# Attention and two MoE layers on one core: weight loads moved behind batch 0's first 256 rows, and the stacked 64-row block transposed once per pair of heads

## The chip, the cores and the metric

The kernel runs on one core of a Trainium2 chip. The metric is device time in microseconds (us), the median of several executions of the compiled program; lower is better.

## What is computed

```python
# q, k, v: (4, 8, 576, 64), f: (4, 8, 576)
scores = q @ k.T / 8
cum = cumsum(log(clip(f, 1e-4, 1)))
scores = where(causal, -1e9, scores + cum[:, None] - cum[None, :])
attn = softmax(scores) @ v
x = attn as (2304, 512)
y = relu(x @ w_in) ** 2 @ w_out        # 512 -> 2048 -> 512
out = elu(y @ w2_in) @ w2_out
```

## The kernel before

Each batch has 8 heads in 4 pairs. A head's 576 rows are five blocks of at most 128, and the work of a pair is cut into steps: two "A" steps (one per head: rows 0 to 255, two blocks), a "4" step (the last 64 rows of both heads, stacked into one block of 128 rows), and two "B" steps (one per head: rows 256 to 511). In batch 0 all eight A steps come first, then "4", "B", "B" for each pair; in the others a pair's five steps follow each other (`todo`, line 651). The loop of line 709 issues step i's scores and softmax (`soft`) and the transposes and products with v of step i - 1 (`outs`).

Batch 0 is computed in full fp32 (`Plain`); the others split each operand in two fp32r parts, so a product is two or three matmuls. The probabilities are transposed on TensorE against an identity (`tr`, line 397), copied out of PSUM (`split_pt`, line 393, by ACT and VectorE) and multiplied with v (`av`, line 400). `out_b` (line 464) does this for a B step: for each 128-column piece J (`turn`, line 473) it transposes the stacked block `e4`, and the head's two blocks in `e`. The stacked block holds both heads, 64 rows each; the identity has 192 columns, and a shift of its columns by 64 puts the half of the current head next to the head's other blocks:

```python
tr(pt[:, 0:128], e4[:, j], last)     # last = 64 * (1 - k)
tr(pt[:, 128:256], e[:, j])
tr(pt[:, 256:384], e[:, 512 + J * 128:640 + J * 128])
```

So both heads of a pair transpose all five pieces of `e4`. `out_a` (line 443) multiplies a second block padded with zeros to 256 columns, `out_b` a fourth one padded to 256.

Beside the attention runs the first half of the first MoE layer. Its rows go in units of 256 (`unit`, line 591): a unit is 18 small steps, 8 of the first product (`ph`), 8 of the second (`o`), and two others. `moe_step` (line 683) issues the next one; a credit of `PACE[b] * COST[kind]` steps per attention step says how often. Unit 0 takes batch 0's first 256 rows and can start when batch 0's A steps are done. All MoE matmuls are issued on line 176 (`mm3`).

The weights arrive as fp64 and are converted on the chip (`load_w`, line 143): 16 halves of 512 KB, first the eight of `w_in`, then the eight of `w_out`. `stage` (line 133) issues the DMA on SP's queue; then ACT takes the absolute value (line 156), VectorE assembles the bits in four operations (lines 157 to 160), ACT rounds to fp32r (line 163) and POOL subtracts for the low part (line 128). `W_AT` (line 36) says how many halves are issued at step i of the loop: one each in steps 0 to 3, two each in steps 8 to 13. The first five DMAs go out at step 0 (line 721).

The decay (`cum`, line 215) is added inside the score matmul: its rows `ca` are written to partitions 64 to 67 of the query and key tiles by DMAs of ACT's queue (line 257). The order of instructions on each engine is then set by the tile framework's scheduler.

Of the kernel before, what the change touches and what calls it, by code (L numbers as in the profile page):

```python
# [10 lines left out]
F32 = mybir.dt.float32  # L11
# [24 lines left out]
W_AT = (1, 1, 1, 1, 0, 0, 0, 0, 2, 2, 2, 2, 2, 2)  # L36
# [14 lines left out]
FOLD = 'vv'  # L51
# [9 lines left out]
BUFS = {'raw': 3, 'qs': 3, 'vv': 4, 'ea': 2, 'eb': 3, 'p': 4, 't': 2, 'x': 1, 'xh': 1}  # L61
# [17 lines left out]
def attention_then_moe_kernel(ctx, tc, first, firstv, plain, qkv, aug0, f, w1, w2, out):  # L79
# [18 lines left out]

    ident = const.tile([128, 192], F32, name="ident")
    make_identity(nc, ident[:, 0:128])  # L100
    nc.gpsimd.tensor_copy(ident[:, 128:192], ident[:, 0:64])
# [28 lines left out]
    staged = []  # L130
# [12 lines left out]
    def load_w(src, m, fc, wp, i, late):  # L143
# [17 lines left out]
        if not late:  # L161
            stage()
# [38 lines left out]
    ptA = [[a1.tile([128, 512], F32R, name=f"ptA{s}{t}") for t in range(2)] for s in range(2)]  # L201
    ptB = [[a1.tile([128, 320], F32R, name=f"ptB{s}{t}") for t in range(2)] for s in range(2)]
    e4s = [a1.tile([128, 640], F32, name=f"e4_{s}") for s in range(2)]
# [21 lines left out]
    for s in range(2):  # L225
        for t in range(2):
            me.memset(f32(ptA[s][t][:, 384:512]), 0.0)
            nc.gpsimd.memset(f32(ptB[s][t][:, 256:320]), 0.0)
        nc.gpsimd.memset(e4s[s][:, S:640], 0.0)
# [148 lines left out]
    def soft_4(b, hp, hhs):  # L378
        e = e4s[hp % 2]
# [17 lines left out]
    def tr(dst, src, c0=0):  # L397
        seen[0] = nc.tensor.transpose(dst, src, ident[:, c0:c0 + 128])  # L398
# [8 lines left out]
    def fold(pv, n, x, c0, k, eng, hh=None):  # L407
        if isinstance(hh, Plain):
            copy(eng, x[64 * k:64 * k + 64, c0:c0 + n], pv[0:64, 0:n])
# [3 lines left out]
        if eng == "v":  # L413
            nc.vector.tensor_tensor(x[64 * k:64 * k + 64, c0:c0 + n], pv[0:64, 0:n], t[:, 0:n], op=ALU.add)
        else:
            u = ab.tile([64, 320], F32, tag="t", name="u", bufs=BUFS["t"])
            nc.scalar.activation(out=u[:, 0:n], in_=pv[0:64, 0:n], func=AF.Copy)
            nc.gpsimd.tensor_tensor(out=x[64 * k:64 * k + 64, c0:c0 + n], in0=u[:, 0:n], in1=t[:, 0:n], op=ALU.add)
# [24 lines left out]
    def out_a(hh, e, x, k):  # L443
# [13 lines left out]
        split_pt(pt[:, 0:384], hl[0][:, 0:384], hl[1][:, 0:384])  # L457
# [3 lines left out]
        av(pv[:, 0:256], hh, 1, [t[:, 256:512] for t in hl], False, True)  # L461
        fold(pv, 256, x, 0, k, FOLD[0])

    def out_b(hh, e, e4, x, k):
        last, near = 64 * (1 - k), 64 * k
        native = isinstance(hh, Plain)

        def unsplit(pt, n, J):
            p = ab.tile([128, 320], F32, tag=f"p{J % 2}", name="pp", bufs=BUFS["p"])
            copy(CP["pB"][J % 2], p[:, 0:n], pt[:, 64:64 + n])  # L470
            return [p]

        def turn(J):
            j = slice(J * 128, J * 128 + 128)
            pt = ps_t.tile([128, 512], F32, tag="t", name="pt")
            if J < 3:
                tr(pt[:, 0:128], e4[:, j], last)
                tr(pt[:, 128:256], e[:, j])
                tr(pt[:, 256:384], e[:, 512 + J * 128:640 + J * 128])
                if native:  # L480
                    return unsplit(pt, 320, J)
                hl = [ab.tile([128, 320], F32R, tag=f"p{t}", name=f"p{t}", bufs=BUFS["p"]) for t in range(2)]
                split_pt(pt[:, 64:384], hl[0], hl[1])
            else:
# [3 lines left out]
                if native:  # L488
                    return unsplit(pt, 256, J)
# [454 lines left out]
```

## Time and profile before

| | |
|---|---|
| median of 3 executions | 1054.24 us (1053.77 to 1060.94) |
| the profiled execution | 1059.11 us, its span 1057.3 us |
| TensorE matmul, weight load | 1031.7 us (98%), 877.4 us (83%) |
| VectorE, ACT, POOL | 617.1 us (58%), 492.4 us (47%), 226.6 us (21%) |

The engines are called PE (TensorE matmul), PEld (TensorE weight load), DVE (VectorE), ACT, POOL and SP as the profile does. The profiled execution holds the attention from 0 to about 372 us; what follows are the two MoE layers. Durations of matmuls overlap, since they are pipelined: how fast TensorE goes is read from the distance of starts. An fp32 matmul is two records in the trace.

### The profile page before, as it was taken

The numbers are of one execution on the slowest core, as the hardware profiler recorded it, in microseconds if no ns is written. First come the engines' busy times: TensorE is split into PE (matmuls) and PEld (weight loads), VectorE is DVE, ScalarE is ACT, GpSimd is POOL, SyncE is SP. The second block draws the span as 40 slices with busy tenths as digits, with TensorE's granted clock in tenths as the row PEclk, the third lists the DMA queues.
The fourth block names the chain that finished last, engine by engine and source line by source line (L and its number), as shares of the span: only waits on it lengthen the run. The fifth ranks groups of instructions, "written<-read, shape, count | busy, mean of one in ns | idle before, by whom it ended". The sixth has DMA issues, their size and how long they took to land.

```text
span 1057.3 us, 15495 instructions
## 1 busy us (share of the span) xinstructions
PE 1031.7 (98%) x5696; PEld 877.4 (83%) x5696; DVE 617.1 (58%) x1363; ACT 492.4 (47%) x1055; POOL 226.6 (21%) x261
## 2 busy tenths in 40 slices
PE   5999999999999999999999999999999999999998
PEld 3667798999999988889988888888888888888897
DVE  5794478766776548858875278943433433343353
ACT  4675688777786634435443154521222222222232
POOL 3457487675775200000000000000000000000000
PEclk9999999999999999999999999999999999999999
DMA  7762534543431173454747237302100300200010
GB/s 244 205 180 89 182 117 150 173 162 125 153 124 47 43 230 122 122 177 140 238 162 238 80 120 249 110 1 77 42 1 1 120 1 1 73 9 1 0 41 20
DMA packets 60112, 115.48 MB, mean 109 GB/s; under 512 B 7332, under 2 KB 34724, under 8 KB 60004
## 3 DMA queue, kind: packets, MB, share of 16 engines
q1 hardware_dynamic: 59972, 114.42, 33.5%
q8 instruction: 45, 0.74, 0.3%
q14 instruction: 31, 0.25, 0.1%
q10 hardware_dynamic: 64, 0.07, 0.0%
HBM read 87.37 MB, written 27.69 MB: 109 GB/s over the span
## 4 chain that ended last, share of the span: by engine, by line
PE 91%; DVE 4%; ACT 2%; DMA 1%; issue 1%; POOL 1%; ACTq 0%; POOLq 0%
PE O L176 32%; PE pH L176 32%; PE o L176 6%; PE ph L176 5%; PE pt L398 4%; PE pv L405 3%; PE s L326 2%; PE pv L402 2%; PE s L330 2%; PE s L331 2%; DVE wt L159 1%; PE pr L398 1%; ACT qk L119 1%; DVE wt L160 1%; DVE wt L158 1%
## 5 line engine op out<-in xcount | busy, mean ns | idle before, releaser
L176 PE MATMUL pH<-xu,w 128*128 128x512 f32 (+1 forms) x1632 | 354.0, 367 | 0.0
L176 PEld LDWEIGHTS pH<-xu,w 128*128 128x128 f32 x1632 | 283.0, 188 | 55.3
L176 PE MATMUL O<-w,gh 128*128 128x512 f32 x576 | 179.0, 394 | 0.0
L576 ACT ACTIVATE g<-g 128x512 f32<-128x512 f32 (+1 forms) x80 | 47.1, 589 | 197.0 <-DVE g L575 196.6
L176 PEld LDWEIGHTS O<-w,gh 128*128 128x128 f32 x576 | 107.2, 188 | 24.7
L176 PE MATMUL O<-gh,w 128*128 128x512 f32 (+1 forms) x448 | 122.0, 362 | 0.0
L115 DVE TENSOR_TENSOR gl<-g,gh 128x512 fp32r<-128x512 f32 (+1 forms) x136 | 85.1, 627 | 54.3 <-ACT gh L578 44.3
L176 PE MATMUL O<-w,gl 128*128 128x512 f32 x288 | 111.3, 392 | 0.0
L575 DVE TENSOR_SCALAR g<-pH 128x512 f32<-128x512 f32 (+1 forms) x80 | 51.0, 637 | 101.7 <-PE pH L176 101.6
L176 PEld LDWEIGHTS O<-gh,w 128*128 128x128 f32 x448 | 79.8, 189 | 14.2
L128 POOL TENSOR_TENSOR qk<-raw,qk 64x704 fp32r<-64x704 f32 (+1 forms) x48 | 78.8, 1642 | 20.4 <-ACT qk L119 15.2
L176 PE MATMUL O<-gl,w 128*128 128x512 f32 (+1 forms) x224 | 79.4, 363 | 0.0
L176 PE MATMUL o<-gh,w 128*128 128x256 f32 x384 | 76.6, 292 | 1.2 <-DVE xB L430 1.2
L577 DVE SCALAR_TENSOR_TENSOR g<-g,pH 128x512 f32<-128x512 f32 (+1 forms) x80 | 50.7, 634 | 45.7 <-ACT g L576 45.4
L156 ACT ACTIVATE wt<-wraw 128x512 f32<-128x512 f32 x57 | 38.0, 669 | 78.4 <-DMA wraw<-in_w_dram 69.6
L578 ACT ACTIVATE gh<-g 128x512 fp32r<-128x512 f32 (+1 forms) x80 | 47.0, 589 | 56.6 <-DVE g L577 56.6
L176 PE MATMUL ph<-xu,w 128*128 128x256 f32 x480 | 67.3, 287 | 1.6 <-DMA xu<-x 1.3
L176 PEld LDWEIGHTS O<-w,gl 128*128 128x128 f32 x288 | 54.1, 188 | 12.4
L176 PEld LDWEIGHTS ph<-xu,w 128*128 128x128 f32 x480 | 60.7, 190 | 2.5 <-DMA xu<-x 1.7
L176 PEld LDWEIGHTS o<-gh,w 128*128 128x128 f32 x384 | 60.4, 190 | 2.0 <-issue 1.4
L567 ACT ACTIVATE gh<-g 128x512 fp32r<-128x512 f32 (+1 forms) x80 | 46.6, 584 | 27.9 <-DVE g L566 23.8
L157 DVE TENSOR_SCALAR wt<-wt 128x512 f32<-128x512 f32 x64 | 29.2, 456 | 44.7 <-ACT wt L156 31.9
(132 smaller groups left out, 1694.7 us busy)
## 6 DMA issues: line engine op xcount, KB each, us to landing
wraw<-in_w_dram SPq DMA_DIRECT2D x57, 512.0 KB
raw<-in_qkv_dram SPq DMA_DIRECT2D x24, 800.0 KB
xu<-x SPq DMA_DIRECT2D x20, 512.0 KB
x<-xs SPq DMA_DIRECT2D x16, 320.0 KB
xu<-x SPq DMA_DIRECT2D x20, 256.0 KB
x<-yh SPq DMA_DIRECT2D x16, 256.0 KB
x<-yl SPq DMA_DIRECT2D x16, 256.0 KB
raws_w<-in_w_dram SPq DMA_DIRECT2D x7, 512.0 KB
```

What stands on the lines that cost most here:

```text
L115: nc.vector.tensor_tensor(dst, x, f32(hi), op=ALU.subtract)
L128: nc.gpsimd.tensor_tensor(out=dst, in0=x, in1=f32(hi), op=ALU.subtract)
L156: nc.scalar.activation(out=f32(t), in_=f32(hi), func=AF.Abs)
L157: nc.vector.tensor_scalar(f32(t), f32(t), W_MIN, W_MAX, op0=ALU.max, op1=ALU.min)
L176: nc.tensor.matmul(out=dst, lhsT=l, rhs=r, start=first and i == 0, stop=last and i == n - 1, skip_group_check=skip)
L398: seen[0] = nc.tensor.transpose(dst, src, ident[:, c0:c0 + 128])
L405: seen[0] = nc.tensor.matmul(out=dst, lhsT=hh[2][:, J, :], rhs=hl[i], start=first and i == 0, stop=last and i == 1)
L567: nc.scalar.activation(out=gh[:, 0:n], in_=g[:, 0:n], func=AF.Copy)
L575: nc.vector.tensor_scalar(g[:, 0:n], h[:, 0:n], 0.0, None, op0=ALU.min)
L576: nc.scalar.activation(out=g[:, 0:n], in_=g[:, 0:n], func=AF.Exp)
L577: nc.vector.scalar_tensor_tensor(g[:, 0:n], g[:, 0:n], -1.0, h[:, 0:n], op0=ALU.add, op1=ALU.max)
L578: nc.scalar.activation(out=gh[:, 0:n], in_=g[:, 0:n], func=AF.Copy)
```

## The change

It moves the weight loads: none in the first eight steps, then one in each of steps 8 to 23, and the first five DMAs go out at step 4. Unit 0's n-th step waits in program order until n halves are loaded, and its second product (from its ninth step) until all 16 are; before, the ninth step issued whatever was left. And it changes `out_b`: head 0 of a pair transposes the stacked block for both heads, next to its own blocks in tiles `P` of up to 640 columns: the order is [two, three, stacked | three, two], so that head 0 reads columns 0 to 319 and head 1 columns 320 to 639. Head 1 only adds its own two blocks. Head 0's result then comes in another order, and is added in three pieces (`fold`). The stacked block and the `P` tiles have one buffer each. The zero padding of the second and fourth blocks goes away.

```diff
-W_AT = (1, 1, 1, 1, 0, 0, 0, 0, 2, 2, 2, 2, 2, 2)
+W_AT = (0, 0, 0, 0, 0, 0, 0, 0, 1, 1, 1, 1, 1, 1, 1, 1, 1, 1, 1, 1, 1, 1, 1, 1)
...
     def stage():
-        if not to_stage:
+        n = n_raw[0] % 5 if n_raw[0] < 10 else n_raw[0] % 2
+        if not to_stage or n in held:
             return
         fc, i = to_stage.pop(0)
-        n = n_raw[0] % 5
         n_raw[0] += 1
+        held.append(n)
...
-    e4s = [a1.tile([128, 640], F32, name=f"e4_{s}") for s in range(2)]
+    e4t = a1.tile([128, 640], F32, name="e4t")
...
     def out_a(hh, e, x, k):
...
-        av(pv[:, 0:256], hh, 1, [t[:, 256:512] for t in hl], False, True)
+        av(pv[:, 0:128], hh, 1, [t[:, 256:384] for t in hl], False, True)
...
     def out_b(hh, e, e4, x, k):
...
         def turn(J):
-            j = slice(J * 128, J * 128 + 128)
+            if k == 0:
+                w = 640 if J < 3 else 512
+                turned[J] = [ab.tile([128, w], F32 if native else F32R, tag=f"P{J}{t}", name=f"P{J}{t}", bufs=1) for t in range(parts)]
             pt = ps_t.tile([128, 512], F32, tag="t", name="pt")
+            three_, four_ = (y[:, J * 128:J * 128 + 128] for y in (e, e4))
+            two_ = e[:, 512 + J * 128:640 + J * 128] if J < 3 else None
             if J < 3:
-                tr(pt[:, 0:128], e4[:, j], last)
-                tr(pt[:, 128:256], e[:, j])
-                tr(pt[:, 256:384], e[:, 512 + J * 128:640 + J * 128])
...
+                srcs = [two_, three_, four_] if k == 0 else [three_, two_]
             else:
...
+                srcs = [e4[:, 512:640], three_, four_] if k == 0 else [three_]
+            for i, src in enumerate(srcs):
+                tr(pt[:, i * 128:i * 128 + 128], src)
+            n = 128 * len(srcs)
+            c = slice(0, n) if k == 0 else slice(384, 384 + n)
...
-                av(pv[:, 0:320], hh, J, hl, J == 0, False)
+                av(pv[:, 0:320], hh, J, [t[:, 320 * k:320 * k + 320] for t in hl], J == 0, False)
             else:
-                n3 = 192 if native else 256
-                av(pv[:, 0:n3], hh, 3, [t[:, 64:64 + n3] for t in hl], False, False)
-                av(pv[:, 0:64], hh, 4, [t[:, 0:64] for t in hl], False, True)
-                fold(pv, 320, x, 0, k, CP["xB"] if native else FOLD[1], hh)
+                av(pv[:, 128 - 128 * k:320 - 128 * k], hh, 3, [t[:, 128 + 192 * k:320 + 192 * k] for t in hl], False, False)
+                c = 0 if k else 256
+                av(pv[:, c:c + 64], hh, 4, [t[:, 64 * k:64 * k + 64] for t in hl], False, True)
+                fold(pv, 320, x, 0, k, CP["xB"] if native else FOLD[1], hh, [(0, 0, 320)] if k else [(0, 192, 128), (128, 64, 128), (256, 0, 64)])
...
     def moe_step():
...
+            if not u and loaded[0] < (16 if n_step[0] >= 9 else n_step[0]):
+                return False
...
-            n_step[0] += 1
-            if n_step[0] == 9:
-                drain(wl)
+            if not u:
+                n_step[0] += 1
...
-        if i == 0:
+        if i == 4:
             for _ in range(5):
                 stage()
...
         for _ in range(W_AT[i] if i < len(W_AT) else 0):
             next(wl, None)
+            loaded[0] += 1
```

How this moves instructions is seen at three places. The first is the head of SP's queue (`fr` is the decay input, `rawA` the queries and keys of a pair's first 256 rows, `raws_w` and `wraw` the weights). Before:

```order
6 L255 DMA rawA<-in_first_dram 64x1024
7 L258 DMA rawA<-in_firstv_dram 128x256
8 L140 DMA raws_w<-in_w_dram 128x1024 x2
9 L140 DMA wraw_181<-in_w_dram 128x1024
10 L140 DMA wraw_183<-in_w_dram 128x1024
11 L140 DMA wraw_185<-in_w_dram 128x1024
12 L711 DMA aug<-in_aug_dram 16x2560
13 L255 DMA rawA<-in_first_dram 64x1024
```

Afterwards:

```order
6 L250 DMA rawA<-in_first_dram 64x1024
7 L253 DMA rawA<-in_firstv_dram 128x256
8 L705 DMA aug<-in_aug_dram 16x2560
9 L250 DMA rawA<-in_first_dram 64x1024
10 L253 DMA rawA<-in_firstv_dram 128x256
11 L279 DMA aug<-ca 8x2x256 x2
12 L279 DMA aug<-cp 8x2x256
13 L279 DMA aug<-cp 8x2x64
14 L279 DMA aug<-cn 8x2x320
15 L139 DMA wraw_265<-in_w_dram 128x1024
```

Five weight DMAs left the place ahead of the fourth pair's input; three now stand behind the decay rows, two more (`raws_w`) further down.

The second place is TensorE in the last two pairs of batch 0 (`pr` turns the sums of a pair, `pv` are products with v, `s` scores, `pt` transposes). Before, from the end of the third pair:

```order
122 L398 MATMUL pr<-ident,rb 128x128 x2
123 L176 MATMUL o<-gl,w_1_207 128x256
124 L326 MATMUL s<-rawB 128x384
125 L176 MATMUL o<-gh,w_2_242 128x256 x2
126 L176 MATMUL o<-gl,w_2_242 128x256
127 L176 MATMUL o<-gh,w_2_242 128x256 x2
128 L176 MATMUL o<-gl,w_2_242 128x256
129 L176 MATMUL o<-gh,w_3_294 128x256 x2
```

Afterwards, from the last `ph` of unit 0 on:

```order
106 L176 MATMUL ph<-x_116,w_7_838 128x256 x12
107 L393 MATMUL pr<-ident,rb 128x128 x2
108 L397 MATMUL pv<-P_707,vp 64x320
109 L397 MATMUL pv<-P_732,vp 64x320
110 L321 MATMUL s<-rawC 128x512
111 L397 MATMUL pv<-P_740,vp 64x320
112 L397 MATMUL pv<-P_747,vp 64x192
113 L397 MATMUL pv<-P_747,vp 64x64
114 L321 MATMUL s<-rawC 128x384
115 L393 MATMUL pt<-ident,eb 128x128 x2
```

No `o` stands between the attention's matmuls any more; the first one is in row 199, among batch 1's first pairs.

The third is TensorE in the last pair of batch 1 (`e_1` or `e4t` is the stacked block, `eb` a head's own two). Before, the transposes of one head, each piece with the stacked block:

```order
606 L398 MATMUL pt<-ident,e_1_130 128x128
607 L398 MATMUL pt<-ident,eb 128x128 x2
608 L405 MATMUL pv<-p_2368,vv 128x320
609 L405 MATMUL pv<-p_2369,vv 128x320
610 L405 MATMUL pv<-ptB_125,vv 128x256
611 L398 MATMUL pt<-ident,e_1_130 128x128
612 L398 MATMUL pt<-ident,eb 128x128 x2
```

Afterwards, those of a head 1:

```order
513 L393 MATMUL pt<-ident,eb 128x128 x2
514 L325 MATMUL s<-qk_2071 128x384
515 L326 MATMUL s<-qk_2072 128x384
516 L400 MATMUL pv<-P_2150,vv 128x320
517 L400 MATMUL pv<-P_2178,vv 128x192
518 L393 MATMUL pt<-ident,eb 128x128 x2
519 L400 MATMUL pv<-P_2179,vv 128x192
520 L400 MATMUL pv<-P_2178,vv 128x64
```

A head 1 has no transposes of the stacked block left, and its fourth block's products have 192 columns.

## Rows read from the trace of the kernel before

**Rows 1.** The page's 40 slices of the span: granted TensorE clock, in tenths.
```profile
PEclk9999999999999999999999999999999999999999
```
**Rows 2.** Stretches: start:end, length, PE, PEld, DVE, ACT, POOL busy, clock, DMA, GB/s.
```profile
46.00:88.00 42.00, 40.32 (x220) 28.50 (x219) 39.38 (x88) 31.55 (x73) 23.16 (x23) 1.00 0.51 147
88.00:129.00 41.00, 41.00 (x251) 30.40 (x249) 15.31 (x54) 22.31 (x52) 21.89 (x25) 1.00 0.47 158
131.00:208.00 77.00, 72.69 (x554) 68.56 (x554) 59.86 (x185) 64.13 (x165) 57.59 (x63) 1.00 0.43 141
208.00:284.00 76.00, 76.00 (x622) 75.27 (x621) 51.10 (x152) 57.49 (x142) 54.45 (x60) 1.00 0.45 148
```
**Rows 3.** The same stretch, 88 to 129 us, line 176 alone: PE, PEld busy.
```profile
88.00:129.00 41.00, 16.93 (x108) 13.68 (x106) 1.00 0.47 158
```
**Rows 4.** Timeline of the first 10 us: SP's and ACT's queues, VectorE.
```profile
0.74 0.39 SPq L196 DMA_DIRECT2D fr<-in_f_dram  x1
...
2.63 0.81 DVE L210 TENSOR_SCALAR fr<-fr 32x576 f32<-32x576 f32 x1 [2.63 <-DMA fr<-in_f_dram]
...
5.66 2.94 SPq L140 DMA_DIRECT2D wraw<-in_w_dram  x3
...
7.46 5.90 ACTq L257 DMA_DIRECT2D rawA<-ca  x5
```
**Rows 5.** Timeline of TensorE, 12 to 62 us: start, us, engine, line, what.
```profile
12.85 5.46 PE L326 MATMUL s<-rawA 68*128 68x256 f32 x12 [12.85 <-DMA rawA<-ca]
18.10 1.06 PE L398 MATMUL pt<-ident,ea 128*128 128x128 f32 x4
18.95 1.92 PE L326 MATMUL s<-rawA 68*128 68x256 f32 x4
...
46.51 1.63 PE L176 MATMUL ph<-x,w 128*128 128x256 f32 x6
48.07 1.54 PE L402 MATMUL pv<-ea,rawA 128*64 128x256 f32 x4
...
50.83 0.86 PE L402 MATMUL pv<-ea,rawA 128*64 128x256 f32 x4
...
54.15 0.58 PE L176 MATMUL ph<-x,w 128*128 128x256 f32 x1
...
59.19 0.27 PE L398 MATMUL pt<-ident,e 128*128 128x128 f32 x1
59.30 0.38 PE L398 MATMUL pt<-ident,eb 128*128 128x128 f32 x2
...
61.90 0.58 PE L176 MATMUL ph<-x,w 128*128 128x256 f32 x1
```
**Rows 6.** The tile `wt` of a weight load: duration min/median/max in ns.
```profile
L157 DVE TENSOR_SCALAR wt<-wt x16: 414/422/1408, 15.6 to 81.2; 128x512 f32<-128x512 f32 x16
...
L163 ACT ACTIVATE w<-wt x16: 612/629/649, 19.4 to 85.7; 128x512 fp32r<-128x512 f32 x16
L128 POOL TENSOR_TENSOR w<-wt,w x16: 1259/1272/1452, 20.5 to 86.4; 128x512 fp32r<-128x512 f32 x16
L156 ACT ACTIVATE wt<-wraw x9: 645/668/688, 21.8 to 76.0; 128x512 f32<-128x512 f32 x9
L159 DVE SCALAR_TENSOR_TENSOR wt<-wraw,wt x9: 664/694/1664, 24.4 to 79.1; 128x512 int32<-128x512 int32 x9
```
**Rows 7.** Timeline of TensorE, 215 to 235 us.
```profile
215.96 0.63 PE L405 MATMUL pv<-ptA,vv 128*128 128x256 f32 x4
216.43 0.52 PE L176 MATMUL ph<-xu,w 128*128 128x256 f32 x3
...
229.10 0.42 PE L405 MATMUL pv<-ptB,vv 128*128 128x256 f32 x3
229.36 0.55 PE L398 MATMUL pt<-ident,ea 128*128 128x128 f32 x3
```
**Rows 8.** Groups by line and form, VectorE, 120 to 380 us.
```profile
L414 DVE TENSOR_TENSOR xB<-pv,t 64x320 f32<-64x320 f32 x24 | 11.6, 482 | 7.3 <-ACT t L412 6.7
```

More of the change, by code (lines that the diff above doesn't have):

```diff
@@ L161, in load_w @@
         if not late:
+            held.pop(0)
             stage()
@@ L200, in attention_then_moe_kernel @@
     m4 = a1.tile([128, 288], F32, name="m4")
-    ptA = [[a1.tile([128, 512], F32R, name=f"ptA{s}{t}") for t in range(2)] for s in range(2)]
-    ptB = [[a1.tile([128, 320], F32R, name=f"ptB{s}{t}") for t in range(2)] for s in range(2)]
-    e4s = [a1.tile([128, 640], F32, name=f"e4_{s}") for s in range(2)]
+    ptA = [[a1.tile([128, 384], F32R, name=f"ptA{s}{t}") for t in range(2)] for s in range(2)]
+    e4t = a1.tile([128, 640], F32, name="e4t")
     me = getattr(nc, MEM)
@@ L224, in attention_then_moe_kernel @@
     split_c(ca[:, 0:2, 0:256], ca[:, 2:4, 256:512], slice(0, 256))
[L225 to L229, printed above, removed]
+    nc.gpsimd.memset(e4t[:, S:640], 0.0)
     nc.gpsimd.memset(m4, 0.0)
@@ L378, in soft_4 @@
     def soft_4(b, hp, hhs):
-        e = e4s[hp % 2]
+        e = e4t
         nm, z, r = (ab.tile([128, 1], F32, tag=t + "1", name=t + "1", bufs=3) for t in ("nm", "z", "r"))
@@ L395, in split_pt, with tr @@
         nc.vector.tensor_tensor(lo, pt, f32(hi), op=ALU.subtract)
-    def tr(dst, src, c0=0):
-        seen[0] = nc.tensor.transpose(dst, src, ident[:, c0:c0 + 128])
+    def tr(dst, src):
+        seen[0] = nc.tensor.transpose(dst, src, ident)
     def av(dst, hh, J, hl, first, last):
@@ L405, in av, with fold @@
             seen[0] = nc.tensor.matmul(out=dst, lhsT=hh[2][:, J, :], rhs=hl[i], start=first and i == 0, stop=last and i == 1)
-    def fold(pv, n, x, c0, k, eng, hh=None):
+    def fold(pv, n, x, c0, k, eng, hh=None, pieces=None):
+        rows = slice(64 * k, 64 * k + 64)
+        pieces = pieces or [(0, c0, n)]
         if isinstance(hh, Plain):
-            copy(eng, x[64 * k:64 * k + 64, c0:c0 + n], pv[0:64, 0:n])
+            for f, c, m in pieces:
+                copy(eng, x[rows, c:c + m], pv[0:64, f:f + m])
             return
@@ L412, in fold @@
         nc.scalar.activation(out=t[:, 0:n], in_=pv[64:128, 0:n], func=AF.Copy)
[L413 to L418, printed above, removed]
+        for f, c, m in pieces:
+            nc.vector.tensor_tensor(x[rows, c:c + m], pv[0:64, f:f + m], t[:, f:f + m], op=ALU.add)
     def norm_x(b, hp, kind, x, c0):
@@ L456, in out_a @@
         hl = ptA[k]
-        split_pt(pt[:, 0:384], hl[0][:, 0:384], hl[1][:, 0:384])
+        split_pt(pt[:, 0:384], *hl)
         yield
@@ L460, in out_a @@
         av(pv[:, 0:256], hh, 0, [t[:, 0:256] for t in hl], True, False)
-        av(pv[:, 0:256], hh, 1, [t[:, 256:512] for t in hl], False, True)
+        av(pv[:, 0:128], hh, 1, [t[:, 256:384] for t in hl], False, True)
         fold(pv, 256, x, 0, k, FOLD[0])
+    turned = {}
     def out_b(hh, e, e4, x, k):
-        last, near = 64 * (1 - k), 64 * k
         native = isinstance(hh, Plain)
[L468 to L471, printed above, removed]
+        parts = 1 if native else 2
@@ L492, in turn @@
-            return hl
-        hls = [turn(0)]
+                srcs = [two_, three_, four_] if k == 0 else [three_, two_]
+            else:
+                srcs = [e4[:, 512:640], three_, four_] if k == 0 else [three_]
[3 more added lines that the diff above has]
+            c = slice(0, n) if k == 0 else slice(384, 384 + n)
+            if native:
+                copy(CP["pB"][J % 2], turned[J][0][:, c], pt[:, 0:n])
+            else:
+                split_pt(pt[:, 0:n], *(t[:, c] for t in turned[J]))
@@ L495, in out_b @@
+        turn(0)
         yield
-        hls.append(turn(1))
+        turn(1)
         yield
@@ L681, in attention_then_moe_kernel @@
     n_step = [0]
+    loaded = [0]
     def moe_step():
```

24 lines of the change are left out of this document (6 added, 18 removed).

## The prediction

> **What bounds the kernel now.** The page comes first: TensorE has nearly all the busy time, and its row of granted clock is full in every slice [rows 1]. Since matmuls are pipelined, their durations overlap and a busy share near 100% doesn't say that TensorE has no room; the room shows in how often a matmul starts. So the next view is the table by stretches [rows 2]. In batch 2 (208 to 284 us) 622 records of TensorE start in 76 us, one per 0.122 us. In batch 1 (131 to 208 us) it is 554 in 77 us, one per 0.139 us, with the same kinds of instruction: 77 - 554 x 0.122 = 9.4 us of that stretch are not TensorE's. So batch 2 is bound by TensorE (I take batch 3 as like it) and batch 1 only mostly so. In batch 0 the causal blocks from row 256 on (the "B" steps) fall in two halves: from 46 to 88 us VectorE is busy for 39.4 of 42 us, and TensorE starts only 220 records; from 88 to 129 us VectorE is busy for 15.3 of 41 us and TensorE starts 251 records, 108 of them MoE matmuls of line 176 [rows 3].
>
> Third, the timeline of the start [rows 4, 5]. The decay rows `ca` are written to the query tiles by DMAs from 7.46 us on, and TensorE's first matmul waits for one of them until 12.85 us. From there TensorE is dense, but slow: four transposes take from 18.10 to 18.95 us, 0.21 us each, while from 59.19 to 59.30 us one takes 0.11. The four records of a `pv` group have a span of 1.54 us from 48.07 and 0.86 us from 50.83. The column of granted clock reads 1.00 in all of these stretches, so the level is read from the intervals: 1.2 GHz up to about 50.8 us, 2.4 GHz after. What TensorE did before it rose: 33 us of scores with 68 rows, transposes and 64-column products, almost without a gap, and then, from 46.51 us, the first MoE matmuls.
>
> **The start.** Before, five weight DMAs of 512 KB stand on SP's queue ahead of the fourth pair's input and beside the `ca` DMAs; afterwards none does until the decay rows are out. The first `ca` DMA takes 12.85 - 7.46 = 5.4 us from issue to use. A lone DMA, that of `fr`, takes 2.63 - 0.74 = 1.9 us [rows 4]. So the gain lies between 0 (if the `ca` transfers are slow by themselves) and 5.4 - 1.9 = 3.5 us. I take 3.0, near the row of the lone DMA, since the five weight DMAs are the only large traffic that goes away. The rest of the first 256 rows gains nothing: TensorE is dense there, and the four weight conversions that leave were beside it. They are what ACT, VectorE and POOL no longer do then; they come back later.
>
> **The weights.** One load costs ACT 0.67 + 0.63 us, VectorE two operations of 0.42 and two of 0.69 (2.2 us), and POOL 1.27 us [rows 6]. Of the 16 loads, before: 4 in batch 0's A steps, 12 in the first six steps of the B part (two each). Afterwards: 0, then 6 in the first two pairs of the B part, 6 in the last two, 4 in the first four steps of batch 1. The first eight MoE steps keep their places (one weight each), the other eight need all 16 loads and so move behind the 23rd step: the order shows no MoE matmul in the last two pairs of batch 0.
> - First two pairs: six loads fewer take 6 x 2.2 = 13 us from a VectorE that was busy for 39.4 of 42 us. TensorE is the next in line, and it has little room, so of the 13 I count 2.0 us (0 to 6).
> - Last two pairs: of 41 us, the 108 MoE matmuls took 108 x 0.122 = 13 us; they are not lost but run later, in a dense stretch, at the same price, so moving them costs nothing as long as the stretch gets 13 us shorter. What is left for TensorE is 28 us, less ten transposes: 27. But six loads come in: ACT 22.3 + 7.8 = 30 us (less some 2 of MoE work that leaves), VectorE 15.3 + 13.2 = 28.5, POOL 21.9 + 7.6 = 29.5 (again less 1 or 2). All four engines then need 27 to 29 us, in fixed orders, with each waiting for the others. The stretch can't be under 27 us (1 us better than neutral) and, if it stays at 41, costs 13. I take 31 us, 3.0 over neutral, because in the half before VectorE did reach 39.4 of 42 us with the same kind of mix.
> - Batch 1: four loads in its first pair, ACT 5.2 us, in a stretch where ACT, at 64 of 77 us, is not the bound [rows 2]. Cost 0 to 5.2 us; I take 1.0.
>
> **The transposes.** Before, each head of a pair transposes the five 128-column pieces of the stacked block, with an identity shifted by 64 so that its own half lands beside its other blocks. Afterwards head 0 of a pair does it for both: 5 transposes fewer per pair, 80 in all, 20 per batch. The price is the interval, 0.11 us [rows 5], not the span of one instruction (0.27 us at the same place): spans overlap. 80 x 0.11 = 8.8 us. Two matmul shapes shrink in batches 1 to 3: 48 second products of an A step from 256 columns to 128, and 48 of the fourth block from 256 to 192. Four of 256 columns take from 215.96 to 216.43, 0.118 each; the last three of a fourth block, one of 256 columns and two of 64, take from 229.10 to 229.36, so 64 columns take 0.07 [rows 7]. A 128-column one lies between; the 64-column ones look bound by something other than their columns, so I take 0.07 for 128 (saves 0.048) and 0.094 for 192 (saves 0.024): 48 x 0.048 + 48 x 0.024 = 3.5 us, bounds 0 and 4.6. In all 12.3 us of TensorE: 2.2 in batch 0, 3.4 in each of batches 1 to 3. Where TensorE bounds, that is the gain: batches 2 and 3 give 6.8 (3.4 to 6.8), the first two pairs of batch 0 give 1.1, the last two are counted above, and batch 1, with its 9.4 us of other waits, gives half: 1.7 (0 to 3.4).
>
> A rule of the Trainium skill ("TensorE: Matmul & The Clock Gate", Part 4: PE-mode transpose) puts a transpose at some 275 ns in a kernel's context; by it the 80 would be worth 22 us and the sum below 13 us lower. The timeline has that figure too, as the span of one transpose (0.27 us at 59.19), and the next one starts 0.11 us later, so the measured interval decides.
>
> **What else it moves.** The copies out of PSUM change their shapes, not their columns: per pair eight of 320 or 256 become eight of 384, 256 or 128. The last addition of head 0 is in three pieces: the one of 320 columns takes 0.48 us [rows 8], three take at most 1.4, so under 1 us of VectorE per pair, in stretches where VectorE is busy for 60 of 77 and 51 of 76 us; no cost. Two buffers become one. The stacked block `e4t` of the next pair is written by VectorE (the first row minimum) after head 0's five transposes, and the transposed `P` tiles by ACT and VectorE after head 1's products. Behind that minimum on VectorE stand copies of `P` and a weight's steps, for which TensorE and ACT wait. In batches 1 to 3 two A steps lie between; in batch 0 one step, and I take 0, bound 4 x 5 x 0.11 = 2.2 us.
>
> **The sum.** Start -3.0; first two pairs -2.0 and -1.1; last two pairs +3.0; batch 1 -1.7 and +1.0; batches 2 and 3 -6.8: -10.6 us. The rows are of an execution of 1059.1 us (span 1057.3), 0.5% above the median of 1054.2; the terms are differences of short stretches, so they are taken off the median: 1043.6 us.
>
> **Rivals.**
> - *The clock falls in the last two pairs.* There TensorE has only the mix with which it stayed at 1.2 GHz from 12.85 to 50.8 us: no MoE matmul for some 30 us. For it: that the clock did not rise for 38 us, and rose soon after the first MoE matmuls [rows 5]. Against it: between the MoE matmuls at 54.15 and 61.90 us TensorE had the same mix alone, and the transposes at 59.19 still took 0.11 us. A fall and a rise need not have one condition. Price: 27 us of TensorE at half rate are 54, 23 over the 31 taken: 1067 us. It decides as soon as the clock falls in the first half of the stretch (over 12 us more: slower than before). The Trainium skill speaks for it: the same Part 4 says that transposes do not count as TensorE being busy in the way other matmuls do; the trace agrees for the slow start and not for the 7.7 us from 54.15. Chance 0.10.
> - *The last two pairs keep their length.* Softmax, copies and loads go through three strict queues, and a chain from ACT to VectorE to ACT to POOL stands in each load; the 13 us of MoE are then only put off: +13 in place of +3, 1053.6, no change. For it: those MoE matmuls needed nothing there and were the filler of just such waits. Against it: ACT and VectorE were busy for only half of that stretch. Chance 0.17.
> - *Every bound falls well.* Start -3.5, first pairs -6 and -1.1, last pairs -1.1, batch 1 -3.4 with no cost, batches 2 and 3 -6.8: -21.9, 1032 us. For it: fillers are spread more evenly in batches 1 to 3. Against: batch 1 had room on TensorE already. Chance 0.13.
> - *My sum*, 1037 to 1050: 0.60.
>
> A measurement of this kernel can tell about 1% from no change, here 10.5 us: faster means under 1043.7. A little over half of my own case lies there (0.34) and all of the third rival (0.13): 0.47. The clock gives 0.09 beyond 1% slower; the remaining 0.44 is within 1%. The range 1032 to 1058 takes in the second rival and the lower half of the third, and leaves out the clock.
>
> **What would show it.** Right: first matmul near 9.9 us; VectorE well under 39 of 42 us in the first two pairs; the last two pairs of batch 0 in about 31 us with no line-176 matmul and transposes still 0.11 us apart; pairs of batches 2 and 3 0.85 us shorter each for the same number of MoE matmuls. Wrong: a first matmul still after 12 us, transposes 0.21 us apart after 55 us, or TensorE waiting on ACT, POOL or VectorE between batch 0 and batch 1 for more than some 6 us.

## The result, and the profile after

The changed kernel takes 1065.44 us in the median of 8 executions (1061.25 to 1069.21), the kernel before 1058.68 beside it on the same chip (8 executions); the ratio of all these executions is put at 1.0077 (that of the two medians is 1.0064), its 95% interval 1.0055 to 1.0099. So the change costs some 0.8%, where 1% faster had been forecast, and the time lies above the stated range, which ended at 1058. The profiled execution after is the fastest of its eight (1061.25 us, span 1059.4), that of before was near the top of its range, so the two traces stand only 2.1 us apart. The 97 executions of the kernel before that ran beside the experiments fall in two groups, 61 up to 1056.8 us with a mean granted clock of 0.994 to 0.998 and 36 from 1057.9 us on, half of them at 1.000, and the traced one (1059.11 us, 1.000) is of the second, so what its clock did need not hold for the others.

The first two views answer to [rows 1, 2]: the row of granted clock, and the stretches. The last two pairs of batch 0 and batch 1 are cut here at the same points of the work in both kernels. The kernel before, by these marks:

```profile
93.00:127.00 34.00, 34.00 (x211) 25.69 (x210) 12.85 (x47) 17.60 (x44) 17.44 (x19) 1.00 0.45 151
127.00:204.00 77.00, 73.16 (x551) 67.89 (x550) 59.56 (x184) 64.22 (x163) 56.25 (x61) 1.00 0.46 151
```

The kernel after, the page's row and the stretches (PE, PEld, DVE, ACT, POOL busy, granted clock, DMA share, GB/s); the first of them, 38 to 77.6 us, holds the first two pairs:

```profile
PEclk9999899999999999999999999999999999999999
...
38.00:77.60 39.60, 38.01 (x209) 26.09 (x207) 36.98 (x75) 27.55 (x65) 23.66 (x22) 1.00 0.54 163
77.60:116.00 38.40, 30.61 (x125) 17.24 (x125) 35.15 (x75) 27.73 (x68) 30.11 (x27) 0.87 0.50 165
116.00:195.00 79.00, 70.99 (x509) 64.07 (x507) 65.22 (x186) 60.93 (x156) 53.12 (x59) 0.98 0.47 155
```

The last two pairs of batch 0 now take longer (38.4 us against 34) for 125 records of TensorE instead of 211: VectorE, which had been busy for 12.85 of 34 us, is busy for 35.15 of 38.4. The clock is no longer full there (0.87). With one place on the timeline as the mark (the `pr` transposes that close a pair), the two traces compare so; the last column counts each MoE record of line 176 that a stretch has fewer (or more) than before at the 0.122 us of the prediction:

| stretch | before: us, MoE records | after | forecast | measured, MoE put off counted |
|---|---|---|---|---|
| start to the third pair of A steps | 45.80, 0 | 30.73, 0 | -3.0 | -15.1 |
| to the end of the second B pair | 47.33, 107 | 46.86, 96 | -3.1 | +0.9 |
| last two pairs of batch 0 | 33.98, 85 | 38.44, 0 | +3.0 | +14.8 |
| batch 1 | 76.91, 192 | 78.81, 180 | -0.7 | +3.4 |
| batches 2 and 3 | 166.51, 669 | 169.12, 698 | -6.8 | -0.9 |
| in all | 370.53, 1053 | 363.95, 974 | -10.6 | +3.1 |

The start, against [rows 4, 5]: the first matmul comes at 10.85 us (before 12.85), and four records of a `pv` group have a span of 1.46 us at 19.69 and 0.86 at 21.62, so in this execution the clock rises at about 21 us; before, the same pair of rows stands at 48.07 and 50.83.

```profile
7.41 4.62 ACTq L252 DMA_DIRECT2D rawA<-ca  x6
...
10.85 7.20 PE L321 MATMUL s<-rawA 68*128 68x256 f32 x16 [10.85 <-DMA rawA<-ca]
...
19.69 1.46 PE L397 MATMUL pv<-ea,rawA 128*64 128x256 f32 x4
21.62 0.86 PE L397 MATMUL pv<-ea,rawA 128*64 128x256 f32 x4 [0.47 <-ACT xA L117]
```

The weight loads, against [rows 6]: the tile `wt` from 77 to 118 us alone (minimum/median/maximum in ns). The minima are the old ones, but the medians of three of VectorE's four steps are now 0.87, 0.99 and 0.91 us, where they had been 0.42 and 0.69.

```profile
L156 DVE TENSOR_SCALAR wt<-wt x6: 403/416/1520, 77.3 to 113.4; 128x512 f32<-128x512 f32 x6
L157 DVE TENSOR_SCALAR wt<-wt x6: 417/868/1530, 77.7 to 114.6; 128x512 int32<-128x512 int32 x6
L158 DVE SCALAR_TENSOR_TENSOR wt<-raws_w,wt x6: 660/988/1314, 79.8 to 116.1; 128x512 int32<-128x512 int32 x6
L159 DVE SCALAR_TENSOR_TENSOR wt<-raws_w,wt x5: 681/914/1723, 81.1 to 107.2; 128x512 int32<-128x512 int32 x5
```

What makes them long is seen when the timelines of VectorE and POOL are laid side by side. VectorE, 84 to 90 us:

```profile
83.95 0.68 DVE L329 CUSTOM_DVE_ANT_0 eb<-s,mz 128x512 f32<-128x512 f32 x1
...
85.40 1.52 DVE L121 CAST qk<-qk 64x576 fp32r<-64x576 f32 x1
86.85 0.54 DVE L329 CUSTOM_DVE_ANT_0 eb<-s,mz 128x384 f32<-128x384 f32 x1
...
88.74 1.52 DVE L156 TENSOR_SCALAR wt<-wt 128x512 f32<-128x512 f32 x1 [0.54 <-ACT wt L155]
```

POOL in the same time:

```profile
83.44 1.49 POOL L558 TENSOR_TENSOR g<-g 128x512 f32<-128x512 f32 x1
84.89 1.72 POOL L126 TENSOR_TENSOR w<-wt,w 128x512 fp32r<-128x512 f32 x1
86.56 3.41 POOL L126 TENSOR_TENSOR qk<-raw,qk 64x704 fp32r<-64x704 f32 x2
```

The weight step L156 (0.42 us when alone) begins at 88.74 inside POOL's subtraction for a head of batch 1 and ends at 90.26, 0.29 us after POOL's at 89.97. The cast ends at 86.92, 0.3 after POOL's `w` at 86.61. The row minimum at 83.95, which reads PSUM, takes its usual 0.68 us beside POOL's `g`. Over all 64 steps of the 16 loads: 24 overlap no POOL operation and take 1.01 times 0.415 or 0.685 us in the mean, 40 do and take 1.98 times; before, it was 31 at 1.01 and 33 at 1.69. A load thus cost VectorE 54.5/16 = 3.4 us, and 2.9 before, not 2.2. Row minima of 512 columns, which read PSUM, take 0.68 us in the mean of the 23 that overlap a POOL operation and 0.68 in that of the 9 that do not.

The Trainium skill ("SBUF — State Buffer", Who interferes with whom) says that VectorE and GpSimd share a pair of ports, which one instruction holds to its end while the other is fully blocked, and that a VectorE instruction with at most one SBUF input outside the fast two-port modes isn't concerned. These rows agree on both halves: the held steps end 0.3 us behind POOL's operation, and the row minima keep their time. It is the rule that the prediction should have weighed.

Who waits, TensorE from 77.6 to 116 us:

```profile
PE s L321 <- DVE nm L329: 3.1, 3, 1.5
PE pt L393 <- DVE P L121: 2.8, 1, 2.8
PE s L325 <- DVE nm L329: 1.6, 1, 1.6
```

And the clock, in three stretches where it fell. Each fall comes 1 to 2 us behind such a wait (1.52 us until 87.45, 2.83 until 104.20, and in batch 1 1.96 until 156.55). The wait alone does not decide it: one of 1.95 us until 175.59 in this trace, and one of 1.68 until 87.53 in that of before, left the clock full.

```profile
89.00:93.00 4.00, 4.00 (x12) 1.43 (x9) 4.00 (x8) 1.21 (x4) 3.84 (x4) 0.57 0.50 154
106.00:113.00 7.00, 5.59 (x14) 3.05 (x15) 5.54 (x15) 2.55 (x8) 6.03 (x7) 0.52 0.18 77
157.00:161.00 4.00, 3.88 (x17) 3.67 (x18) 3.18 (x10) 1.61 (x6) 3.92 (x4) 0.57 0.55 180
```

At 0.5 TensorE runs on its lower level, 1.2 GHz. From 21 us on, 13.7 us of the attention lie there; before, none after 51 us.

### The profile page after: what moved, and what is told of

Its sections match the earlier page's. It is cut to its first block, busy times and chain, and to the rows that moved or that the text cites. A ratio compares the mean times of both kernels' runs of the same rounds, so it can differ in the third digit from the quotient of the medians.

```text
span 1059.4 us, 15365 instructions
## 1 busy us (share of the span) xinstructions
PE 1021.9 (96%) x5616; PEld 864.2 (82%) x5616; DVE 631.4 (60%) x1387; ACT 492.4 (46%) x1063; POOL 228.4 (22%) x251
## 4 chain that ended last, share of the span: by engine, by line
PE 83%; DVE 9%; DMA 3%; issue 3%; ACT 1%; POOL 1%; SPq 0%; ACTq 0%; DVEq 0%; POOLq 0%
PE O L176 32%; PE pH L176 32%; PE o L176 5%; PE ph L176 5%; PE pv L400 3%; PE pt L393 3%; DVE eb L329 2%; PE s L325 1%; DVE qk L121 1%; PE s L326 1%; DMA rawA<-ca 1%; DVE wt L159 1%; PE pv L397 1%; DVE wt L158 1%; DMA raws_w<-in_w_dram 1%
## 5 line engine op out<-in xcount | busy, mean ns | idle before, releaser
L176 PE MATMUL o<-gh,w 128*128 128x256 f32 x384 | 74.2, 290 | 0.0
L176 PEld LDWEIGHTS O<-w,gl 128*128 128x128 f32 x288 | 54.1, 188 | 12.4
L156 DVE TENSOR_SCALAR wt<-wt 128x512 f32<-128x512 f32 x64 | 32.4, 507 | 46.0 <-ACT wt L155 45.5
```

Source lines behind the costliest of these rows:

```text
L156: nc.vector.tensor_scalar(f32(t), f32(t), W_MIN, W_MAX, op0=ALU.max, op1=ALU.min)
L176: nc.tensor.matmul(out=dst, lhsT=l, rhs=r, start=first and i == 0, stop=last and i == n - 1, skip_group_check=skip)
```

## The experiments

"Idle" is the length of a stretch less its matmul records at the distance that each shape has in a dense row (transposes 0.108 us, others by their columns), so time lost at half the clock counts as idle too. All ratios are to the kernel before, run on the same chip beside each experiment. One execution of each is traced, and it need not be a typical one: those of e1 (1064.12 us) and e4 (1055.79) are the slowest of their ten, that of e12 (1050.05) the fastest of its nine.

### The two halves of the change alone

e1: the changed kernel with the load schedule of before. e2: the kernel before with the load schedule, gate and DMAs of after.

```diff
-W_AT = (0, 0, 0, 0, 0, 0, 0, 0, 1, 1, 1, 1, 1, 1, 1, 1, 1, 1, 1, 1, 1, 1, 1, 1)
+W_AT = (1, 1, 1, 1, 0, 0, 0, 0, 2, 2, 2, 2, 2, 2)
-        if i == 4:
+        if i == 0:
```

> Only the transposes: the weight loads stand where the kernel before has them. First theory (the time was lost by the moved loads, since VectorE's steps of a load are stretched where POOL works beside them): 8 to 12 us under the kernel before, the last two pairs of batch 0 as short as before (some 33 us), TensorE's idle time there under 4 us. Rival A (the moved MoE steps leave TensorE without a filler): the same for this kernel. Rival B (the single buffers of the stacked block and of the tiles P hold TensorE up): no faster than the kernel before, with waits of the first matmuls of a head 0 on VectorE in the trace.

> Only the weight loads moved: out_b transposes the stacked block for each head, as before. First theory and rival A: 13 to 20 us slower than the kernel before, with the last two pairs of batch 0 at 38 us or more. Rival B: within 3 us of the kernel before, since the buffers are double again. Aside: if the early rise of the clock (near 21 us in place of 50) comes from taking the loads out of the first eight steps, it is here too.

e1: 1059.76 us, ratio 1.0036 (1.0020 to 1.0053). e2: 1070.16, 1.0128 (1.0083 to 1.0173; four executions). Both halves lose, the loads most; rival B was not wholly wrong. They do not add: alone they cost some 4 and 13.5 us by the ratios, together 8, so on top of the moved loads the transposes seem to take time off (the intervals of e2 and of the change overlap). In e1 TensorE's work falls by 12.4 us until the end of the attention, as forecast (12.3), but its idle time grows by 17.5: in batches 1 to 3 from 12 to 28 us. The 10.2 us at half the clock in batch 1 explain 5.1 of that growth at most. The stretches of e1, batch 1 and after:

```profile
133.00:210.00 77.00, 68.97 (x489) 64.50 (x488) 61.39 (x177) 58.53 (x151) 51.09 (x57) 0.93 0.42 141
210.00:372.00 162.00, 158.74 (x1272) 154.68 (x1270) 110.50 (x345) 124.32 (x309) 103.00 (x115) 1.00 0.34 112
```

One of its waits and what follows, on TensorE:

```profile
168.50 0.33 PE L391 MATMUL pt<-ident,eb 128*128 128x128 f32 x1 [1.97 <-DVE P L388]
...
169.45 1.20 PE L398 MATMUL pv<-P,vv 128*128 128x320 f32 x5
170.45 0.41 PE L323 MATMUL s<-qk 128*128 128x256 f32 x1
170.67 0.41 PE L324 MATMUL s<-qk 68*128 68x256 f32 x1
```

and on VectorE:

```profile
164.56 2.00 DVE L121 CAST qk<-qk 64x576 fp32r<-64x576 f32 x1
166.49 1.62 DVE L113 TENSOR_TENSOR xs<-xA,xs 128x256 fp32r<-128x256 f32 x1
168.04 0.74 DVE L388 TENSOR_TENSOR P<-pt,P 128x256 fp32r<-128x256 f32 x2
```

Two SBUF operations, held by POOL's subtractions for `qk` (164.52 to 167.84), stand ahead of the copy that TensorE waits for; 2 us after that wait the scores start 0.22 us apart and not 0.12. Another such wait, of 1.95 us until 189.46, stands ahead of the fall at 190.5; the first fall, at 142.7 us, comes behind a wait of 1.66 us for a DMA. The kernel before has the same meeting at 165.1 to 168 us, but there TensorE waits for 0.92 us and its clock stays full.

### Is it the buffers or the clock? (e9, e10)

e9 is e1 with two stacked blocks; room for it comes from an A step's tile that takes the place of the last `P` tile. e10 is e1 with five transposes per head 1 that nothing reads.

```diff
-    e4t = a1.tile([128, 640], F32, name="e4t")
+    e4s = [a1.tile([128, 640], F32, name=f"e4t{s}") for s in range(2)]
...
+            for i in range(k + k * (J == 3)):
+                tr(pt[:, 256 + i * 128:384 + i * 128], three_)
```

> The transposes alone (as in e1_transposes), but with two buffers for the stacked block again; to make room the transposed tile of a head 0's A step takes the place of the last P tile. In e1 TensorE stood idle for 18 us of batch 1 by the count of its matmuls, where the kernel before has 8, and three stretches of some 3.3 us ran at half the clock. Theory of the buffers: VectorE no longer waits at the stacked block for head 0's transposes (7.5 us in e1), the waits of TensorE on VectorE's P go, the half-clock stretches of batch 1 with them, and the time is 5 to 10 us under e1, so 2 to 6 us under the kernel before. Rival (clock): the stalls of e1 are no longer than the kernel before has them and only less work stands between them: within 3 us of e1, half-clock stretches still there.

> As e1_transposes, but a head 1 makes five transposes of one of its own blocks into PSUM columns that nothing reads, so TensorE has as many transposes again as in the kernel before (80 more than e1, 8.8 us by the interval of 0.11 us), while buffers, copies and order are those of e1. Theory of the clock (less work for TensorE between the stalls is what lets its clock fall): no half-clock stretch in batch 1, and the time within 3 us of e1 in spite of 8.8 us more of matmuls. Theory of the buffers: the half-clock stretches stay, TensorE's waits on VectorE's P stay, and the time is 5 to 9 us over e1.

e9: 1054.94, ratio 0.9985 (0.9965 to 1.0004). e10: 1055.44, 1.0008 (0.9986 to 1.0030). Both bring e1 back to the kernel before; e9's interval lies under e1's, e10's overlaps it. e10 does it with 8.5 us more of work for TensorE: idle in batches 1 to 3 falls from 28 to 17.5 us, and its trace has no microsecond at half the clock from 51 us to the end of the attention. The mean granted clock of its ten executions is 0.992 to 1.000, of e1's 0.989 to 0.995. The stretches of e10:

```profile
133.00:210.00 77.00, 72.70 (x558) 68.36 (x557) 60.10 (x192) 63.71 (x164) 56.18 (x62) 1.00 0.47 151
210.00:372.00 162.00, 160.36 (x1295) 157.21 (x1295) 108.34 (x333) 120.17 (x298) 100.48 (x113) 1.00 0.32 107
```

In e9 the wait of VectorE at the stacked block for head 0's transposes is gone. In e1 it was this row of VectorE's waits:

```profile
DVE e4t L327 <- PE pt L391: 7.5, 8, 1.6
```

TensorE's waits for `P` behind batch 0, e1 and then e10:

```profile
PE pt L391 <- DVE P L388: 3.9, 2, 2.0
PE pt L391 <- DVE P L388: 0.9, 2, 0.5
```

So the single buffer costs e1 some 5 us by the ratios (shown by e9, which also moves an A step's tile). By which waits it does so is not shown. e10 was to tell the waits from the clock behind them and does not: with the single buffer, and with VectorE still waiting 5.4 us at the block, its added transposes took TensorE's two long waits away as well. With two blocks the clock stays full in e9's batch 1, but 20 us of idle time stay in batches 1 to 3, and of 12.4 us of work saved some 2 are left.

### What holds the last two pairs? (e4, e8)

e4 is the changed kernel without VectorE's bit operations in loads 7 to 16, e8 without POOL's low parts for six heads of batch 1.

```diff
+        if late or loaded[0] < 6:
             nc.vector.tensor_scalar(f32(t), f32(t), W_MIN, W_MAX, op0=ALU.max, op1=ALU.min)
...
-        minus(ENG["ql"][w], qk2[0:64, qc], raw[0:64, qc], qk1[0:64, qc])
+        if b == 1 and h < 6:
+            nc.sync.dma_start(out=f32(qk2[0:64, qc]), in_=f32(qk1[0:64, qc]))
```

> The changed kernel without VectorE's four bit operations in loads 7 to 16 (the weights of these loads are the bare high words, so they are wrong numbers; TensorE's, ACT's and POOL's work stays). Between the end of pair 2 and the end of batch 0 (38 us in the changed kernel) some 20 us of VectorE's time go. Theory of VectorE and POOL: the stretch falls to 28 to 32 us, the half-clock stretches there shorten or go, 6 to 12 us in all. Theory of the missing filler: TensorE still has too little to do there, the clock falls again, and the stretch stays over 35 us.

> The changed kernel without POOL's subtractions for the low parts of the queries, keys and values of batch 1's first six heads (the high part is copied in their place by a DMA, so the product leaves the correction out): some 25 us of POOL's work between 80 and 150 us go away, TensorE's work and the loads stay. First theory: VectorE's steps of a load between 80 and 118 us fall from about 0.95 to 0.5 and 0.75 us in the mean, the cast L121 from 1.7 to about 0.6, and the last two pairs from 38 to 30 to 34 us, 6 us or more in all. Rival A: the steps get no shorter or the stretch stays at 37 us or more, since the filler is still missing.

e4: 1050.95 us, ratio 0.9957 (0.9932 to 0.9982); the stretch from 83.1 to 111.8 us is 28.7 us long, at full clock, without one MoE record in it (elsewhere, at 34.9, 150.9 and 171.4 us, it falls in this trace too):

```profile
83.10:111.80 28.70, 26.48 (x127) 15.50 (x126) 14.10 (x51) 22.53 (x56) 24.13 (x26) 1.00 0.52 168
```

e8: 1053.99 us, 0.9995 (0.9972 to 1.0018); the stretch is 32.4 us, 6.8 of them still at half the clock. Three of its rows, VectorE from 78 to 112 us:

```profile
L157 DVE TENSOR_SCALAR wt<-wt 128x512 int32<-128x512 int32 x6 | 5.6, 936 | 0.1
L121 DVE CAST qk<-qk 64x576 fp32r<-64x576 f32 x3 | 2.5, 838 | 0.0
L156 DVE TENSOR_SCALAR wt<-wt 128x512 f32<-128x512 f32 x6 | 2.5, 410 | 0.0
```

L156 is back at 0.41 us in the mean (0.69 in the changed kernel from 78 to 112 us), the cast at 0.84 (1.71); L157 stays long, since three of the six meet POOL's subtraction of the load before. By the ratios some 9 us of the changed kernel's time come back with POOL's work gone, 13 with VectorE's. Both edits also take work away behind the stretch, so not all of that is the stretch's. The filler is not needed for a short stretch at full clock: e4 has none either.

### Other places for the loads (e3, e7, e13, e15, e16)

Only the schedule and the first DMAs move, in the kernel after (e3, e7) and in the kernel before (e13, e15, e16). The lines are those of e3 (first DMAs at step 4), e7 (step 3), e13 and e16 (steps 3 and 0) and e15 (step 2).

```diff
+W_AT = (0, 0, 0, 0, 0, 0, 0, 0, 2, 2, 2, 2, 2, 2, 2, 2)
+W_AT = (0, 0, 0, 0, 2, 2, 2, 2, 1, 1, 1, 1, 1, 1, 1, 1)
+W_AT = (0, 0, 0, 0, 1, 1, 1, 1, 2, 2, 2, 2, 2, 2)
+W_AT = (0, 0, 0, 2, 2, 2, 2, 2, 2, 2, 2)
```

> The changed kernel with two loads in each of steps 8 to 15, so all 16 are in before the last pair of batch 0 and none lies beside POOL's preparation of batch 1's heads beyond its beginning. First theory: VectorE's median step of a load back at 0.42 and 0.69 us, the stretch from the end of pair 2 to the end of batch 0 under 34 us, in all 8 to 14 us under the changed kernel. Rival A: also faster, since the second products of the MoE fill the last pair again; the two part by what the steps of a load take (A: no shorter). Rival B: no better than the changed kernel by more than 3 us.

e3: 1064.88 us, 1.0083 (1.0047 to 1.0119): a miss, no gain. The loads were early in program order, not in time: eight of POOL's `w` still lie from 75.6 to 112.9 us, beside the preparation of batch 1, and VectorE's L158 has a median of 1.23 us in the group shown (tile `wt`, 77 to 118 us):

```profile
L126 POOL TENSOR_TENSOR w<-wt,w x8: 1275/1326/1704, 75.6 to 112.9; 128x512 fp32r<-128x512 f32 x8
...
L158 DVE SCALAR_TENSOR_TENSOR wt<-wraw,wt x4: 693/1226/2212, 81.7 to 107.2; 128x512 int32<-128x512 int32 x4
```

> The changed kernel with two loads in each of steps 4 to 7 and one in each of steps 8 to 15, the first DMAs issued at step 3 behind the decay rows. POOL has no heads to prepare in batch 0's A steps, so eight loads should cost VectorE 2.2 us each there, and all are in before the last pair. Theory of VectorE and POOL: the first two pairs end near 80 us (77.6 in the changed kernel), the last two take 32 to 36 us with MoE matmuls among them again, 4 to 10 us under the changed kernel. Theory that any load in the A steps keeps the clock at half there: it rises near 45 us in place of 21, and the time is that of the changed kernel or above.

e7: 1054.98 us, 0.9995 (0.9961 to 1.0029), some 9 us under the changed kernel by the ratios. It keeps the early clock (third A pair at 30.51 us), but the last two pairs still take 37.6 us, 36 MoE records among them.

> The kernel before with nothing changed but the time of its loads: the first DMAs at step 3 behind the decay rows, one load each in steps 4 to 7 (before: 0 to 3), then two a step as before. It asks what the empty first steps are worth by themselves. If the early rise of the clock comes from TensorE having no gap in its first 10 us: first matmul near 10.9 us, the clock full from about 21 us, the first two pairs of the B steps ending 7 to 13 us earlier, 6 to 12 us in all under the kernel before. If only the 2 us of the first matmul count: 1 to 3 us under it.

e13: 1062.08 us, 1.0061 (1.0029 to 1.0093): slower, with everything expected of the start in place (third A pair at 30.88 us, 15 earlier). Its last two pairs take 45.7 us. VectorE at their beginning:

```profile
87.89 1.76 DVE L123 CAST qk<-qk 64x576 fp32r<-64x576 f32 x1
89.57 1.61 DVE L157 TENSOR_SCALAR wt<-wt 128x512 f32<-128x512 f32 x1
91.22 0.97 DVE L158 TENSOR_SCALAR wt<-wt 128x512 int32<-128x512 int32 x1
92.22 1.63 DVE L159 SCALAR_TENSOR_TENSOR wt<-wraw,wt 128x512 int32<-128x512 int32 x1
93.77 0.68 DVE L334 CUSTOM_DVE_ANT_0 eb<-s,mz 128x512 f32<-128x512 f32 x1
```

Four held operations (2.0 us of work in 5.9) stand ahead of a row minimum; TensorE waits 4.92 us for it, until 94.52, and from 93.1 us on the clock is at half for 10.2. The loads were the old ones; they only met POOL's preparation of batch 1 (from 86.05 us here), which in the kernel before begins at 90.98, behind the last load on POOL (86.4, [rows 6]). So the 15 us won at the start were lost again, 5.6 of them in the first two pairs and 11.7 in the last two, by the marks of the table.

> The kernel before with the weight DMAs at step 0 as they were, but the work of the first four loads in steps 4 to 7 (before: 0 to 3). If the DMAs ahead of the decay rows set the first matmul: it starts near 12.9 us, as before. If the work of ACT, VectorE and POOL in those steps kept the clock low: it rises near 23 us all the same, the A steps end 10 to 14 us earlier, and the total is near e13's. If the DMAs did: the clock rises near 50 us.

e16: 1055.98 us, 0.9995 (0.9975 to 1.0016). The first matmul starts at 12.69 us and the clock rises at about 44 us. The first of these hangs on the DMAs at step 0, as the forecast had it: the work of the loads was gone from steps 0 to 3, and e13, which differs by the place of these DMAs alone, starts at 10.93. The late clock goes with it in these two traces, but whether the DMAs cause it stays open, with one execution of each kernel traced: in the traces with a first matmul by 11.9 us the clock rose by 24 us (e3 alone later), in those from 12.0 us on not before 40, and in four of the first kind it fell once more between 30 and 49 us.

> The kernel before, with e14's loads (first DMAs at step 2, two loads in each of steps 3 to 10) and nothing of the transposes. e14 was 0.7% under the kernel before. If the loads alone make that, 1046 to 1052 here too. If the shared transposes are worth what they cost in TensorE's work in batches 1 to 3 (8 to 10 us) once the stacked block has two buffers: 1055 to 1061. TensorE's idle time by the count of its matmuls should then be smaller in batches 1 to 3 than in e14 (12 us against 22).

e15: 1055.51 us, 0.9989 (0.9968 to 1.0010): these loads alone change nothing.

### Towards a faster one (e11, e12, e14)

e11 is e7 with the two stacked blocks of e9; e12 adds a finer gate; e14 has e15's loads in e12.

```diff
-            if not u and loaded[0] < (16 if n_step[0] >= 9 else n_step[0]):
+            if not u and loaded[0] < (min(16, 2 * n_step[0] - 8) if n_step[0] >= 9 else n_step[0]):
```

> e7_early_two (two loads a step from step 4, then one) with the two buffers for the stacked block of e9. In e7 TensorE stood idle for 22.8 us in batches 1 to 3 by the count of its matmuls (the kernel before: 12). If the single buffer is what costs there, as e9 had it against e1, 4 to 8 us go: 1047 to 1051. If the two don't add, since the stalls of the last two pairs of batch 0 remain as they are: 1052 to 1055.

> e11 with a finer wait in program order: unit 0's n-th step of its second product waits for the halves that it reads (10, 12, 14, 16), not for all 16. The MoE steps of batch 0's last two pairs then come earlier and fill TensorE's waits. Theory of the missing filler: the half-clock stretch near 85 us goes, 2 to 5 us under e11. Theory of VectorE and POOL: the stretch is as long as before, since VectorE sets it, within 2 us of e11.

> e12 with two loads in each of steps 3 to 10 and the first DMAs at step 2, so that all 16 are done before POOL prepares a head of batch 1. Theory of VectorE and POOL: no step of a load over 1 us from 80 us on, the last two pairs of batch 0 in 33 to 36 us with their MoE matmuls, the time 3 to 6 us under e12. Against it: six loads are again in the first two pairs, where VectorE had no room in the kernel before; if they cost as much there, within 2 us of e12.

e11: 1059.94, 1.0031 (1.0000 to 1.0063): a miss; its trace has half-clock stretches from 34 to 44 us and five later ones, and why it has more of them than e7 was not found. e12: 1053.81, 0.9962 (0.9930 to 0.9995); the half-clock stretch at 88 to 95 us is still there. That does not test the theory of the filler: its last two pairs hold 36 MoE records, as in e11, so the gate moved none there. e14: 1050.88, 0.9931 (0.9900 to 0.9962; five executions), faster than both kernels. Its last two pairs:

```profile
83.50:119.40 35.90, 34.02 (x208) 25.04 (x207) 17.26 (x50) 20.42 (x53) 24.53 (x25) 1.00 0.52 172
```

All loads are done at 89 us, VectorE is busy for half of the stretch, 92 MoE records are in it, and the clock is full. Four steps of a load from 80 us on still took over 1 us (up to 1.76), against what was expected. Against e15, which differs by the transposes, the buffers and the gate, 12.6 us less work for TensorE leave some 6 us by the ratios.

## Why the prediction was wrong

- **The last two pairs** failed most: +3.0 forecast, +14.8 measured. The step was the price of a load, "VectorE two operations of 0.42 and two of 0.69 (2.2 us)". It cost 3.4. These are medians of [rows 6]; the maxima in the same rows (1408, 1664 ns) were left unread, and such lengths were the price beside POOL. The prediction put ACT, VectorE and POOL down as three busy times that only wait for each other, but two of them stop each other: from 76 to 118 us 25 weight steps and three casts took 11 us more than alone. That is the size of the 11.8 missing, though not all of it need be on the path. VectorE was busy for 35.2 us where 28.5 had been counted, while ACT (27.7 of 30) and POOL (30.1 of 29.5) came out near the count. TensorE's waits in the stretch come to 8.3 us; over 6 around there had been named as a sign of being wrong. e4 and e8 show it from both sides, e13 once more in the other kernel. The second rival (+13, 1053.6) named the right place and nearly the right size, with another reason.
- **The clock** was a rival, for lack of MoE matmuls. It did fall, for 10 us of that stretch (5.1 us of TensorE's work at most), but behind waits on VectorE; e4, without them and without MoE matmuls, kept it there.
- **The start** was right in its step (the weight DMAs delay `ca`; e16 bears it out) and a third too large: 2.0 us, not 3.0. What nobody forecast is the early clock. It makes up most of the other 13 us of that stretch (an estimate: the 10 us from 21 to 30.7 us would have taken 20 at half the clock). Whether any of it reached the end is not shown, since e13 won as much and lost it again.
- **The first two pairs** were to gain 3.1 us, 2.0 of it from VectorE's relief, and gave none. The step that failed is "six loads fewer": it counted loads by the step that issues them, not by the time at which they run. Between the marks of the table VectorE's steps on `wt` make up 9.25 loads before and 10.25 after, and VectorE was busy for 40.4 of 47.3 us before, for 43.1 of 46.9 after.
- **The transposes** saved the work forecast (12.4 us), at 0.11 us each; the smaller products came out near it (128 columns 0.058 us apart in a dense row, where 0.07 was taken). Two steps failed. "Two buffers become one" was priced at 0; the second stacked block gives e1 some 5 us back (e9). VectorE waits at the single one in batches 1 to 3 too (7.5 us in e1). That these waits reach TensorE through the copies behind them is argued, not shown. And "Where TensorE bounds, that is the gain": batches 2 and 3 gave 0.9 of 6.8 us, and with two blocks and as many MoE records as before they are 4.4 us shorter up to the last `pr` (e9).
- **Batch 1** was to gain 0.7 us and lost 3.4. Next to no load ran there (half a one, where four were counted); TensorE's two waits for `P` (1.96 and 1.95 us) are also in e1 (1.97 and 1.95), whose loads were long done, so they come with the transposes' half of the change.

## What to carry to other kernels

Price an operation by what runs beside it where it will stand, not by the median of the place it leaves: the maximum in a row of durations is a question, and the timelines of VectorE and POOL side by side answer it. On an engine that is nearly full, work that is saved turns into waits unless what it waits for gets faster too, and a wait can cost about its own length once more in the clock behind it (2.83 us here, then 6.8 us at half). Gaining time early shifts all that follows against work that is scheduled elsewhere, so look at what it will then meet.

## What was not expected of the hardware

VectorE's steps of a load between SBUF tiles took 1.5 to 2.0 times as long in a kernel's mean where POOL worked beside them (0.42 became up to 1.53 us in the changed kernel), and a cast of 0.45 us up to 2.0, while the row minima and copies that read PSUM kept their time. TensorE's clock fell to the lower level, for 3 to 14 us, during a wait of 1.0 to 4.9 us or within some 2 us behind one; other waits of such lengths left it full (1.68 us in the kernel before, 1.95 in the changed one, 2.17 in e13), so the length of one wait did not tell which. And 80 transposes that nothing needs (e10) made e1 some 3 us faster by the ratios, 4 by the medians. In the traced executions the first matmuls ran for 10 us at the lower level in some kernels and for over 25 in others, with little between them but a start 1 to 2 us later; why was not found.
